# Rows of maxima by four turnings and two transfers, maxima 20 steps ahead, products of the first dense group among the second block's transpositions

## The chip, the core and the metric

The kernel runs on one core of a Trainium2 chip. The metric is the device time of one execution in microseconds (us). Five engines work beside each other, each on its own list of instructions in order: TensorE (PE: matrix products; PEld: the loading of their weights), VectorE (DVE), ScalarE (ACT), GpSimd (POOL) and SyncE (SP, which issues nearly all transfers here).

## The reference

The input x has 2048 rows of 512. It is normalised to xn, and two branches are multiplied: attention with 32 heads of 16 that share one key head and one value head, and a dense layer pair with Mish between.

```
xn = layernorm(x)                              # 2048 x 512
q  = xn @ wq  (32 heads of 16);  k = xn @ wk;  v = xn @ wv      # one k, one v
p  = softmax(q k^T / 4)  over 2048 keys, for each head
s  = concat(p v) @ wo                          # 512 x 512
h  = xn @ w1 + b1                              # 1792 wide
a  = h * tanh(softplus(h))
g  = silu(a @ w2)
out = x + s * g
```

## The kernel before, in words

Queries are cut into four chunks of 512, heads into eight groups of four. One chunk with one group of heads is a *vector* v here; there are NU = 32 of them. A vector's scores are made twice.

- *Maxima* (`m_one`, product L1118, reduction L1122): queries on the partitions, 512 keys a product. DVE reduces each product to one maximum per row. A vector has 64 of them: on each of two sides a (partitions 0 to 63 and 64 to 127) 32.
- *Scores* (`score`, product L1090, exponential L1095): keys on the partitions, 512 queries a product; ACT takes the exponential. 64 a vector. The softmax needs the maximum subtracted, and it comes in through the product itself: two more rows of the query tile `qt` (row 48 and 49 of each side) hold the negated maximum in two parts, and the key tile holds ones there.

`c_rows(v)` brings the maxima of a vector into these rows, in four pieces: `reduce` (the last maximum over four key blocks), `parts` (two instructions that split it), `turn` (DVE's transposition in blocks of 32x32, from queries on the partitions to queries along the row; L1151) and `move` (SP transfers from `cr` into `qt`, L1161). The first score of a vector waits for them.

The loop over 512 *steps* (16 a vector) issues in each step four scores, four value products (`pv`, L1176; each shows as two instructions in the trace) and the four maxima (two a side) of a vector LEAD steps ahead, so with LEAD = 22 the maxima of vector v end 6 steps ahead of its first score. Between them it lays the *dense* products (`xps`: query projections, both dense layers and the output projection). Inside the loop they run as two halves of 64 rows on the two sides, 4, 6 or 8 halves a step (`waves`), or 16 halves in two steps of a *unit* of four steps (`unit`), or none where no dense group is ready. `top_rows` issues one piece of `c_rows` a step (two per half unit). The last LEAD steps (`tail_pair`, two steps a pair) have no maxima.

Ahead of the loop stands a *lead*: normalisation, transpositions of x (`xp`, L315, four blocks of 512 rows: c = 0 to 3), key and value projections (`kp`, L356), the first query projections and 2 x LEAD maxima a side. A planner lays it out as it builds the program: each task has an engine, a cost and its predecessors; the planner keeps a clock T for each engine and issues the task that can start earliest. Kind "M" is a pair of maxima, kind "X" up to three dense products in whole (L118), and where nothing is ready it issues a product whose result is not used (`keep_warm`, L1431 before). A task with `fill=True` (transpositions of blocks 1 to 3) gets a `keep_warm` in front if no dense group is open. When the 32 maxima a side of vector 0 are issued, the planner sets tasks for `c_rows(0)` and the time `cdone` at which its rows will have landed; the lead ends at `cdone` less 0.4 us, and not before `min(m_next)` reaches 2 x LEAD.

Tile names in the rows: `qt` queries, `ks` keys, `m` and `e` the products of maxima and scores, `mb` the maxima, `mp` their parts, `cr` the turned rows, `pts` exponentials (and at the start x), `xps`, `wop` and `y2ps` banks of dense products, `hb` the first dense layer's output, `ws`, `wq`, `wbs` weights in two parts, `raw*` weights as loaded.

## Time and profile before

| | |
|---|---|
| median of 3 runs | 1561.91 us (1559.70 to 1562.19) |
| profiled execution, its own time | 1561.58 us |
| its span, first to last instruction | 1559.8 us |
| mean granted TensorE clock | 0.998 of full speed |
| busy: PE, DVE, ACT, POOL | 99%, 86%, 83%, 41% of the span |
| maxima, scores, value products | 2048, 2048, 2048 (x2 in the trace) |
| reduction of one maximum (L1122), mean | 683 ns listed |
| exponential of one score (L1095), mean | 607 ns listed |

The profile is one execution. A row of the timeline merges like instructions in a row; its length counts to the end of the last, while the next row may start before that, since instructions overlap by part of their length. The time that a row costs the engine is therefore the distance from its start to the next row's. Starts are counted from the first instruction of the span. In brackets stands how long the engine stood idle ahead of the row, and what ended that.

### The profile page before, as it was taken

The numbers are of one execution on the slowest core, as the hardware profiler recorded it, in microseconds if no ns is written. First come the engines' busy times: TensorE is split into PE (matmuls) and PEld (weight loads), VectorE is DVE, ScalarE is ACT, GpSimd is POOL, SyncE is SP. The second block draws the span as 40 slices with busy tenths as digits, with TensorE's granted clock in tenths as the row PEclk, the third lists the DMA queues.
The fourth block names the chain that finished last, engine by engine and source line by source line (L and its number), as shares of the span: only waits on it lengthen the run. The fifth ranks groups of instructions, "written<-read, shape, count | busy, mean of one in ns | idle before, by whom it ended". The sixth has DMA issues, their size and how long they took to land.

```text
span 1559.8 us, 31423 instructions
## 1 busy us (share of the span) xinstructions
PE 1548.8 (99%) x11715; PEld 864.1 (55%) x11715; DVE 1348.1 (86%) x2280; ACT 1292.6 (83%) x2509; POOL 636.3 (41%) x668
## 2 busy tenths in 40 slices
PE   9999999999999999999999999999999999999998
PEld 6555655655555565565545556555554555655644
DVE  7998888889989988888998988888889999888854
ACT  6588888789888778977989788897788878878796
POOL 4787349366356203331625422163152323314122
PEclk9999999999999999999999999999999999999999
DMA  6334134133231303212113220321321213131020
GB/s 199 104 133 139 46 111 139 30 113 112 87 111 49 108 16 113 72 24 100 52 58 111 92 92 17 104 69 58 111 59 38 100 58 105 30 99 32 19 71 34
DMA packets 71955, 125.47 MB, mean 80 GB/s; under 512 B 19742, under 2 KB 33356, under 8 KB 71804
## 3 DMA queue, kind: packets, MB, share of 16 engines
q1 hardware_dynamic: 71372, 122.68, 24.9%
q8 instruction: 93, 1.52, 0.4%
q10 hardware_dynamic: 432, 0.79, 0.1%
q14 instruction: 58, 0.48, 0.1%
HBM read 75.57 MB, written 26.21 MB: 65 GB/s over the span
## 4 chain that ended last, share of the span: by engine, by line
PE 98%; DVE 1%; ACT 0%; DMA 0%; issue 0%
PE xps L122 45%; PE pv L1176 32%; PE m L1118 10%; PE e L1090 7%; PE xps L118 1%; DVE mb L1122 1%; PE warm L1344 1%; PE kp L356 0%; PE xp L315 0%; PE wop L122 0%; ACT pts L1095 0%; PE y2ps L122 0%; DMA ks<-ks 0%; PE wop L118 0%; ACT hb L808 0%; ACT xt L324 0%
## 5 line engine op out<-in xcount | busy, mean ns | idle before, releaser
L1122 DVE TENSOR_REDUCE mb<-m 128x1 f32<-128x512 f32 x2048 | 1266.2, 683 | 164.2 <-PE m L1118 129.0
L1095 ACT ACTIVATE pts<-e 128x512 f32<-128x512 f32 x2048 | 1064.8, 607 | 218.3 <-PE e L1090 164.0
L1118 PE MATMUL m<-ks,qt 48*128 48x512 f32 (+1 forms) x2048 | 842.3, 422 | 1.2 <-DMA ks<-ks 1.2
L1090 PE MATMUL e<-qt,ks 64*128 64x512 f32 x2048 | 750.9, 406 | 0.2 <-ACT pts L1095 0.2
L1176 PE MATMUL pv<-pts,vaug 128*32 128x512 f32 x4096 | 529.9, 603 | 0.0
L1118 PEld LDWEIGHTS m<-ks,qt 48*128 48x128 f32 (+1 forms) x2048 | 371.1, 185 | 79.5 <-DVE mb L1122 41.4
L1090 PEld LDWEIGHTS e<-qt,ks 64*128 64x128 f32 x2048 | 375.8, 186 | 29.9 <-ACT pts L1095 16.3
L122 PE MATMUL xps<-wbs,act 64*128 64x512 f32 x1270 | 324.6, 399 | 0.0
L122 PE MATMUL xps<-xt,ws 64*128 64x512 f32 x1128 | 312.3, 409 | 1.7 <-ACT pts L1095 0.9
L122 PEld LDWEIGHTS xps<-xt,ws 64*128 64x128 f32 x1128 | 194.4, 185 | 185.7 <-ACT pts L1095 123.3
L122 PEld LDWEIGHTS xps<-wbs,act 64*128 64x128 f32 x1270 | 227.0, 184 | 99.5 <-ACT pts L1095 26.8
L1176 PEld LDWEIGHTS pv<-pts,vaug 128*32 128x32 f32 x4096 | 88.3, 108 | 152.5 <-issue 144.5
L175 POOL TENSOR_TENSOR hb<-hb,t 128x512 f32<-128x512 f32 x56 | 72.2, 1289 | 163.2 <-ACT t L827 89.4
L185 POOL TENSOR_SCALAR t<-t 128x512 f32<-128x512 f32 x56 | 34.4, 614 | 181.5 <-ACT t L814 181.4
L122 PE MATMUL xps<-xt,wq 64*128 64x512 f32 x336 | 93.0, 409 | 0.0
L122 PEld LDWEIGHTS xps<-xt,wq 64*128 64x128 f32 x336 | 57.9, 185 | 55.4 <-ACT pts L1095 37.7
L175 POOL TENSOR_TENSOR oc<-oc,sc 128x512 f32<-128x512 f32 (+1 forms) x16 | 20.6, 1290 | 152.5 <-DMA qt<-qh 49.8
L122 PE MATMUL xps<-wbs,ot_all 64*128 64x512 f32 x288 | 79.3, 408 | 0.0
L122 PEld LDWEIGHTS xps<-wbs,ot_all 64*128 64x128 f32 x288 | 49.5, 184 | 46.9 <-ACT pts L1095 28.5
L175 POOL TENSOR_TENSOR act<-hb,act 128x512 fp32r<-128x512 f32 x56 | 72.1, 1288 | 4.7
L175 POOL TENSOR_TENSOR hb<-hb,u 128x512 f32<-128x512 f32 x56 | 72.2, 1289 | 4.4
L175 POOL TENSOR_TENSOR u<-u,t 128x512 f32<-128x512 f32 x56 | 71.9, 1284 | 4.7
(164 smaller groups left out, 878.6 us busy)
## 6 DMA issues: line engine op xcount, KB each, us to landing
wbs<-w SPq DMA_DIRECT2D x39, 512.0 KB
ws<-w SPq DMA_DIRECT2D x36, 512.0 KB
qt<-qh SPq DMA_DIRECT2D x256, 32.0 KB
w<-wbs SPq DMA_DIRECT2D x14, 512.0 KB
wq<-wq SPq DMA_DIRECT2D x14, 512.0 KB
wbs<-wo SPq DMA_DIRECT2D x12, 512.0 KB
rawws<-in_dram SPq DMA_DIRECT2D x20, 256.0 KB
w<-ws SPq DMA_DIRECT2D x10, 512.0 KB
```

The source lines that it names most:

```text
L118: self.pe.matmul(ps, self.lhs(), self.rhs(), start=(self.k == 0), stop=(self.k == self.tot - 1))
L122: i = self.pe.matmul(ps, self.lhs()[o], self.rhs()[o], start=(self.k == 0 and self.halves == 0), stop=(self.k == self.tot - 1 and self.hal ...
L175: eng.tensor_tensor(out=o, in0=a, in1=b, op=op)
L185: pool.tensor_scalar(o, o, lim, 0.0, op0=ALU.min, op1=ALU.max)
L1090: pe.matmul(e, ks[o:o + 64, P * k:P * (k + 1)], q[o:o + 64, p], start=True, stop=True)
L1095: x = act.activation(dst, e, AF.Exp, scale=0.25)
L1118: pe.matmul(m, q[o, p, P * t:P * (t + 1)], ks[o, C * kb:C * (kb + 1)], start=True, stop=True)
L1122: return dve.reduce_max(out=mb_of[v][:, kb, z:z + 1], in_=m, axis=AX.X)
L1176: pe.matmul(o[32 * j:32 * j + 32], vaug[:, k], pt, start=(k == 0), stop=(k == 15))
L1344: pe.matmul(warm, qts[0][:, 0, 0:P], qts[0][:, 0], start=True, stop=True)
```

## The change

Four things change. LEAD goes from 22 to 20 (with a term of the query projections' due time adjusted so that it stays where it was). `turn` becomes four transpositions of 32 partitions each, that write side by side into a tile of 32 partitions x 128, in place of one of 128 x 32. `move` needs two transfers a vector (one a side, of 16 rows of 512 bytes) in place of eight of 16 rows of 128 bytes. And in the planner a dense product is issued ahead of each `fill` task while a dense group is open and its clock stands below 27.0 us; the costs of `c_rows(0)` in the planner follow the new forms.

```diff
-LEAD = 22
+LEAD = 20
...
-                     [lambda: 32 * (4 * c + b) - LEAD - 18, lambda: xt_done.get(c)])
+                     [lambda: 32 * (4 * c + b) - LEAD - 20, lambda: xt_done.get(c)])
...
         def turn():
-            cr = w["cr"] = sb.tile([P, 32], F32, tag="cr", name=f"cr{v}", bufs=2)
-            dve.transpose(cr, f(mp[:, :, 1:3]).rearrange("p a s z -> p a (s z)"))
+            cr = w["cr"] = sb.tile([32, P], F32, tag="cr", name=f"cr{v}", bufs=2)
+            for b in range(4):
+                z = slice(32 * b, 32 * b + 32)
+                dve.transpose(cr[:, z], f(mp[z, :, 1:3]).rearrange("p a s z -> p a (s z)"))
...
             for a in range(1, -1, -1):
                 r = 64 * a + 48
-                for b in range(4):
-                    sp_at(0.68)
-                    sp.dma_start(f(q[r:r + 2]).rearrange("o p (t b n) -> b o (p t) n", b=4, n=32)[b],
-                                 cr[32 * b + 16 * a:32 * b + 16 * a + 16])
+                sp_at(0.68)
+                sp.dma_start(f(q[r:r + 2]).rearrange("o p (t n) -> o (p t) n", n=P), cr[16 * a:16 * a + 16])
...
-                r1 = task("DVE", 0.9, lambda: (r[0](), r[1](), r[2]()))
+                r1 = task("DVE", 1.2, lambda: (r[0](), r[1](), r[2]()))
...
-                    cdone[0] = now[0] + 4 * 0.65 + 2.0
-                task("SP", 5.2, move, [r1])
+                    cdone[0] = now[0] + 2 * 0.65 + 2.0
+                task("SP", 1.3, move, [r1])
...
             plan[e].remove(k)
-            if k.fill and cur["g"] is None and not waiting:
+            if k.fill and cur["g"] is not None and s < 27.0:
+                fill(1)
+            elif k.fill and cur["g"] is None and not waiting:
                 keep_warm()
```

How the order of instructions moves is shown at three places. The first is PE at the end of the lead (`m` maxima, `xps` dense products, L118 in whole and L122 in halves). Before:

```order
L118 MATMUL xps<-xt_175,ws_833 128x512 x3
L1118 MATMUL m_0_8_955<-ks,qt_78 128x512
L1118 MATMUL m_1_8_958<-ks,qt_78 128x512
L1118 MATMUL m_0_9_963<-ks,qt_78 128x512
L1118 MATMUL m_1_9_966<-ks,qt_78 128x512
L118 MATMUL xps<-xt_175,ws_833 128x512 x6
L1118 MATMUL m_0_10_982<-ks,qt_78 128x512
L1118 MATMUL m_1_10_985<-ks,qt_78 128x512
L1118 MATMUL m_0_11_988<-ks,qt_78 128x512
L1118 MATMUL m_1_11_991<-ks,qt_78 128x512
```

And in the changed kernel, with the first rows of the loop behind it:

```order
L118 MATMUL xps<-xt_175,ws_842 128x512 x12
L1431 MATMUL warm<-qt_79 128x512 x2
L122 MATMUL xps<-xt_175,ws_929 128x512
L1118 MATMUL m_1_8_980<-ks,qt_78 128x512
L122 MATMUL xps<-xt_175,ws_929 128x512
L1090 MATMUL e_0_0_1_984<-qt_77,ks 128x512
```

Eight maxima have left the lead; the twelve dense products of that group now follow each other, and two products without use stand where the first dense group of the loop waits for its bank.

The second place is SP's queue ahead of the first rows of maxima (`ks<-ks` copies the keys of block 3 to the other side, `raw*` loads weights). Before:

```order
L537 DMA rawws_762<-in_dram 128x4x128
L539 DMA rawwb_774<-in_dram 128x512
L372 DMA ks<-ks 48x256 x2
L537 DMA rawws_881<-in_dram 128x4x128
L1161 DMA qt_77<-cr_911 2x8x32 x8
```

And now:

```order
L537 DMA rawws_775<-in_dram 128x4x128
L372 DMA ks<-ks 48x256 x2
L539 DMA rawwb_792<-in_dram 128x512
L537 DMA rawws_890<-in_dram 128x4x128
L1162 DMA qt_77<-cr_917 2x8x128 x2
```

The copy of the keys has moved ahead of one weight load, and eight transfers have become two.

The third place is PE in the loop, step 8: before, and then in the changed kernel.

```order
L1118 MATMUL m_1_28_1337<-ks,qt_78 128x512
L122 MATMUL xps<-xt_175,xtw 128x512
L1090 MATMUL e_8_0_1_1341<-qt_77,ks 128x512
L122 MATMUL xps<-xt_175,xtw 128x512
L1118 MATMUL m_1_29_1345<-ks,qt_78 128x512
L122 MATMUL xps<-xt_175,xtw 128x512
L1090 MATMUL e_8_1_1_1349<-qt_77,ks 128x512
```

```order
L1118 MATMUL m_0_24_1312<-ks,qt_78 128x512
L1090 MATMUL e_8_0_1_1315<-qt_77,ks 128x512
L1118 MATMUL m_0_25_1318<-ks,qt_78 128x512
L1090 MATMUL e_8_1_1_1321<-qt_77,ks 128x512
L1118 MATMUL m_0_26_1324<-ks,qt_78 128x512
L1090 MATMUL e_9_0_1_1327<-qt_77,ks 128x512
```

No dense product lies between them any more; four steps in a row are like that, since the planner has no dense group ready there.

Over the whole program PE's lists differ as follows. Steps with maxima: before 333 with 6 halves, 26 with 4, 4 with 8 and 62 half units with 16; now 331, 26, 4, 62 and the four without any. Pairs of the tail: before eight with 9 or 10 halves, then two with 13 and one with none; now eight with 9 or 10, then two with 18. The lead has 84 dense products in both, 100 maxima up to the loop's first value products before and 92 now, and seven products without use more.

## Rows read from the trace of the kernel before

**Rows 1.** The page: busy us of each engine, then the chain that ended last.

```profile
PE 1548.8 (99%) x11715; PEld 864.1 (55%) x11715; DVE 1348.1 (86%) x2280; ACT 1292.6 (83%) x2509; POOL 636.3 (41%) x668
...
PE 98%; DVE 1%; ACT 0%; DMA 0%; issue 0%
```

**Rows 2.** Timeline, PE, value products, 388:403 and 538:548 us (start, length, line, form).

```profile
394.27 1.06 PE L1176 MATMUL pv<-pts,vaug 128*32 128x512 f32 x8
397.12 1.06 PE L1176 MATMUL pv<-pts,vaug 128*32 128x512 f32 x8
399.82 1.07 PE L1176 MATMUL pv<-pts,vaug 128*32 128x512 f32 x8
...
539.79 1.06 PE L1176 MATMUL pv<-pts,vaug 128*32 128x512 f32 x8
542.86 1.07 PE L1176 MATMUL pv<-pts,vaug 128*32 128x512 f32 x8
```

**Rows 3.** Timeline, PE, end of the lead.

```profile
61.84 0.83 PE L1118 MATMUL m<-ks,qt 64*128 64x512 f32 x4 [1.19 <-DMA ks<-ks]
...
75.21 0.73 PE L1118 MATMUL m<-ks,qt 64*128 64x512 f32 x4
75.88 1.66 PE L118 MATMUL xps<-xt,ws 128*128 128x512 f32 x6
...
79.88 0.50 PE L122 MATMUL xps<-xt,ws 64*128 64x512 f32 x1 [0.78 <-ACT hb L808]
```

**Rows 4.** Timeline, SP's queue, 54 to 78 us.

```profile
58.15 0.33 SPq L539 DMA_DIRECT2D rawwb<-in_dram  x1
58.57 1.15 SPq L372 DMA_DIRECT2D ks<-ks  x2
```

**Rows 5.** Timeline, DVE, 18 to 86 us.

```profile
28.89 3.68 DVE L1122 TENSOR_REDUCE mb<-m 128x1 f32<-128x512 f32 x6 [1.57 <-PE m L1118]
...
56.09 0.85 DVE L175 TENSOR_TENSOR ks<-kp,ks 16x256 fp32r<-16x256 f32 x2
...
62.34 9.66 DVE L1122 TENSOR_REDUCE mb<-m 128x1 f32<-128x512 f32 x16 [0.49 <-PE m L1118]
...
72.76 0.21 DVE L1151 STREAM_TRANSPOSE cr<-mp 128x32 f32<-128x32 f32 x1
```

**Rows 6.** Windows: stretch, its length, busy us of the engines, then PEclk.

```profile
24.00:29.00 5.00, 4.99 (x20) 3.13 (x19) 3.01 (x7) 4.45 (x13) 2.12 (x5) 0.66 0.24 58
```

**Rows 7.** Timeline, DVE, behind the turning of vector 5.

```profile
307.36 4.28 DVE L1122 TENSOR_REDUCE mb<-m 128x1 f32<-128x512 f32 x7 [0.98 <-PE m L1118]
```

**Rows 8.** Timeline, SP's queue, the transfers of vector 5.

```profile
306.40 5.29 SPq L1161 DMA_DIRECT2D qt<-cr  x8
```

**Rows 9.** Timeline, PE, the first score of vector 5.

```profile
313.12 0.40 PE L1090 MATMUL e<-qt,ks 64*128 64x512 f32 x1
```

**Rows 10.** Timeline, PE, value products of the tail, 1518 to 1549 us.

```profile
1525.47 1.92 PE L1176 MATMUL pv<-pts,vaug 128*32 128x512 f32 x16
1529.91 1.92 PE L1176 MATMUL pv<-pts,vaug 128*32 128x512 f32 x16
1534.93 1.92 PE L1176 MATMUL pv<-pts,vaug 128*32 128x512 f32 x16
1539.99 1.92 PE L1176 MATMUL pv<-pts,vaug 128*32 128x512 f32 x16
1544.43 3.64 PE L1176 MATMUL pv<-pts,vaug 128*32 128x512 f32 x32
```

**Rows 11.** Timeline, DVE, the tail, 1518 to 1549 us.

```profile
1520.36 0.69 DVE L882 TENSOR_TENSOR y<-xps,y 128x512 f32<-128x512 f32 x1 [4.08 <-PE wop L122]
...
1525.17 3.34 DVE L1218 RECIPROCAL sc<-sc 64x512 f32<-64x512 f32 x1
...
1537.44 0.69 DVE L175 TENSOR_TENSOR y<-y,e 128x512 f32<-128x512 f32 x1
1548.63 0.42 DVE L1240 COPY os<-pv 128x256 f32<-128x256 f32 x1 [10.50 <-ACT os L1239]
```

## The prediction

> **What bounds the kernel now.** I read the page first: PE is busy 99% of the span and the chain that ended last is PE for 98% [rows 1]. So time is saved only where PE waits, where it does something without use, or where a step costs more than its products. To see which of these the change touches, I counted instructions by step in the two orders and took the price of a step from PE's timeline: the distance between two blocks of value products. A step with 6 dense halves costs 397.12 - 394.27 = 2.85 us, one with 4 costs 399.82 - 397.12 = 2.70, one with 8 costs 542.86 - 539.79 = 3.07 [rows 2]. The two halves from 6 to 8 cost 0.22 (0.11 each, PE's rate), those from 4 to 6 only 0.15, so something beside PE's products sets a floor near 2.7. Then I read the lead, where PE still waits, engine by engine [rows 3 to 6], and the tail, where ACT's exponentials set 4.44 us a pair [rows 10].
>
> **The change part by part.** The sum is made against the profiled execution's own 1561.58 us, 0.33 below the median of the runs; 1559.8 of it is the span and 1.8 lies around it.
>
> *Eight maxima leave the lead.* At its end PE does four maxima in 75.88 - 75.21 = 0.67 us [rows 3], and two such rows go: -1.3. The wait for the bank at 79.88 (0.78, until ACT has emptied it) stays, and the two products without use fit in it. The transfers of vector 0 do not take its place: the turning starts at 72.76 [rows 5], three more turnings add 0.6, two transfers at 5.29 / 8 = 0.66 each [rows 8] end by 75.1, and the loop would now start near 79.88 - 2.5 = 77.4.
>
> *The keys' copy goes ahead of a weight load.* SP issues it at 58.57, right behind a load at 58.15 [rows 4]; its data are there at 56.09 + 0.85 = 56.94 [rows 5], and one load of 0.33, like that at 58.15, still stands in front: 57.3. So it starts 1.3 us earlier, and PE's wait of 1.19 us at 61.84 goes [rows 3]. What is late next is DVE, which gains only its own 0.49 us [rows 5]; the reductions then run 16 in 9.66, or 0.604 each, without a gap. If PE must go at DVE's pace this is worth 0.5; since it has free banks between the two, I take -1.2.
>
> *Products among the transpositions.* [...] Five dense products are moved in front of these transpositions (from later in the lead; five products without use stand there instead). If the clock stays up the gain is at most 1.7 us; if it falls all the same, five products at 1.66 / 6 = 0.28 [rows 3] cost 1.4. DVE's idle 1.57 us at 28.89 [rows 5] is the part that could pass on. But ACT is busy for 4.45 of these 5 us [rows 6], and the maxima over key block 1 need what it makes there, so what PE gains is given back at their first product. I take 0, with -1.7 and +1.4 as ends. [...]
>
> *The loop.* It has two steps more with maxima: four without dense halves come, two with 6 go. A step without any isn't in the trace. It can't be under DVE's four reductions, 4 x 0.604 = 2.42, and hardly over the 2.85 of a step with 6; I take the nearest row, 2.70. That is 4 x 2.70 - 2 x 2.85 = +5.1, between +4.0 and +5.7.
>
> *The tail.* One pair less. Before, the last three intervals are 5.02, 5.06 and 4.44 = 14.52 us, from 1529.91 to 1544.43 [rows 10], for pairs with 13, 13 and no halves. Now two pairs with 18 stand for them; the eight with 9 or 10 stay, at 4.44 each as the one from 1525.47 to 1529.91. 18 halves cost 5.04 + 5 x 0.11 = 5.6. In the last pair ten are free, as the pairs at 4.44 show, and eight cost 0.9: 5.3. So 14.52 becomes 10.9: -3.6. The ends: 5.04 + 4.44 (all free) gives -5.0, 5.6 + 4.44 + 18 x 0.11 = 12.0 (none free in the last) -2.5.
>
> *Four turnings.* One took 0.21 us [rows 5]. Three more are at most 0.6 us of DVE for each of 32 vectors. In units DVE idles 0.98 us right behind the turning [rows 7], which covers it. In a single step DVE has 2.85 - 2.42 = 0.43 of room, and 0.82 for the turning is 0.39 too much; the three banks between PE and DVE hold back 1.8 us of reductions, so the next step makes it up. I take 0.01 a vector, +0.3 in all; the ends are 0 and 31 x 0.39 = +12. [...]
>
> *Two transfers.* Six issues of 0.66 us less for each vector [rows 8] free SP, which isn't on the path: 0. The time that they save is what LEAD = 20 spends. By the order, four vectors are now the tightest, with five maxima between their turning and their first score; vector 5 before has nine and takes 313.12 - 306.40 = 6.7 us from the first issue to its first score [rows 8, 9], with eight transfers in it and no wait. Four maxima are one step, so 6.7 - 2.85 - 0.6 = 3.2 remain. The first side's transfer is 0.66 long; the copy of keys, a larger one, was used 61.84 - 59.72 = 2.1 after its issue ended [rows 3, 4]. Together 2.8: it fits, by 0.4. I take 0, with +4 (four vectors, 1 us each) as the end.
>
> *The end of the tail.* The reciprocal at L1218 now stands behind the last addition to y (L882), which moves from the sixth-last pair to the third-last. Before, 1525.17 to 1537.44 + 0.69 is 13.0 us from that reciprocal to the last gate on y [rows 11]. Now it starts about 0.7 behind the third-last pair's value products (the addition stands 0.7 ahead of them, 1520.36 to 1521.03, and two instructions of 0.7 come first), so it is through at 13.7; DVE's copy for the last vector stands at 1548.63 - 1534.93 = 13.7 by the same count [rows 10, 11], and 1.4 later with the two longer pairs. So it costs nothing, by 1.4 us; +1 if it doesn't hold.
>
> The sum: -1.3 - 1.2 + 0 + 5.1 - 3.6 + 0.3 = -0.7, so **1560.9 us**.
>
> **The rivals.** *Faster: the clock stays up and the lead's gain is kept.* For it: 1.7 us lost at half clock, DVE idle 1.57 us behind it [rows 5, 6], and a step without dense halves may cost 2.42 rather than 2.70 (-1.1). Against it: ACT is full there. Time: 1560.9 - 1.7 - 1.1 = 1558.1.
>
> *Slower: the turnings stall PE.* Place: the single steps in which a vector is turned, where the maxima wait for a bank. Against it: the banks' 1.8 us and DVE's 0.98 in units [rows 7]. For it: 0.39 us over the step. Half of this uncovered, 0.2 x 31 = 6.2, gives 1560.6 + 6.2 = 1566.8. It makes the kernel slower than before from 1.0 / 31 = 0.03 us a vector on.
>
> *The rows come late.* If the transfers land 1 us later than counted, four vectors wait: 1564.9. The last pieces of the tail could add 1 in the same way.
>
> *The change does nothing for the path at all* is only the case in which lead, loop and tail cancel, which the forecast already nearly is.
>
> **How the numbers follow.** What a measurement of this kernel can tell from no change is about 0.2%, 3.1 us: below 1558.8 or above 1565.0. The forecast has 0.60, with its own range of 1558.9 to 1562.9 from the ends of loop and tail. The faster rival has 0.25 (nearly all below 1558.8), the turnings 0.09, the late rows and the tail's end 0.06 (a third above 1565.0). So faster 0.25, same 0.64, slower 0.11, and the range is 1557.3 to 1564.4, which leaves out the far end of either rival.
>
> **What would show it.** In the profile after: PE's gap ahead of the maxima at about 61 us gone, the loop's first score 2 to 3 us earlier; four value-product distances of 2.4 to 2.85 us at steps 8 to 11; the next to last tail distances near 5.6 and 5.3; the granted clock from 24 to 29 us near 1.0 if the products hold it; steps with a turning at 2.85 as before; DVE's copy at the end not waiting for DVE's own reciprocal. The prediction is wrong if steps with a turning grow, if first scores wait for `cr`, or if the first 80 us change by more than 4 us.

## The result, and the profile after

The changed kernel takes 1565.07 us (median of 9 runs, 1564.84 to 1565.51), the kernel before 1559.96 beside it (9 runs, 1559.70 to 1563.39): ratio 1.0026, 95% interval 1.0016 to 1.0036. It is slower by about 0.26%, and 1565.07 lies 0.7 us above the range of the forecast. The profiled execution took 1565.04 us. Four disturbed runs of the experiments (2397.66 us of after_rev, 3572.86 of dup0, 2060.81 and 7013.09 of the kernel before) are in no median below.

The page after, to be read beside [rows 1]: DVE has 19 us more, in 96 instructions more, which are three more turnings for each of 32 vectors; PE stays at 99%.

```profile
PE 1551.0 (99%) x11722; PEld 862.5 (55%) x11722; DVE 1366.9 (87%) x2376; ACT 1295.0 (83%) x2509; POOL 637.8 (41%) x668
```

The timeline of PE at the end of the lead (start, length, line, form, idle time ahead in brackets) answers to [rows 3]: four maxima at 60.04 without the wait of 1.19 us, and the loop's first product at 77.00 in place of 79.88.

```profile
60.04 0.73 PE L1118 MATMUL m<-ks,qt 64*128 64x512 f32 x4
...
76.45 0.49 PE L1431 MATMUL warm<-qt 128*128 128x512 f32 x1 [0.54 <-ACT hb L808]
77.00 0.49 PE L122 MATMUL xps<-xt,ws 64*128 64x512 f32 x1
```

The window of the transpositions answers to [rows 6]: the granted clock (third number from the end) is 1.00 where it was 0.66.

```profile
24.00:29.00 5.00, 4.89 (x26) 3.07 (x25) 3.73 (x6) 4.92 (x15) 1.74 (x3) 1.00 0.18 43
```

The value products on PE's timeline answer to [rows 2] and [rows 10]. The four steps without dense halves take 3.04, 3.23, 2.71 and 2.71 us; the last two pairs, with 18 halves each, 5.18 and 5.19.

```profile
98.80 1.07 PE L1176 MATMUL pv<-pts,vaug 128*32 128x512 f32 x8
101.84 1.06 PE L1176 MATMUL pv<-pts,vaug 128*32 128x512 f32 x8
105.07 1.07 PE L1176 MATMUL pv<-pts,vaug 128*32 128x512 f32 x8
...
1537.52 1.92 PE L1176 MATMUL pv<-pts,vaug 128*32 128x512 f32 x16
1542.70 1.92 PE L1176 MATMUL pv<-pts,vaug 128*32 128x512 f32 x16
...
1547.89 3.64 PE L1176 MATMUL pv<-pts,vaug 128*32 128x512 f32 x32
```

The time is lost in a place that the forecast held free. A single step that holds a vector's turning is longer in 20 of 31 vectors. Here are DVE and then PE in one of them.

```profile
1272.88 2.48 DVE L1122 TENSOR_REDUCE mb<-m 128x1 f32<-128x512 f32 x4
1275.29 0.83 DVE L1153 STREAM_TRANSPOSE cr<-mp 32x32 f32<-32x32 f32 x4
1276.05 2.43 DVE L1122 TENSOR_REDUCE mb<-m 128x1 f32<-128x512 f32 x4
1278.73 1.29 DVE L1122 TENSOR_REDUCE mb<-m 128x1 f32<-128x512 f32 x2 [0.25 <-PE m L1118]
1280.05 0.69 DVE L175 TENSOR_TENSOR y<-xps,y 128x512 f32<-128x512 f32 x1
```

```profile
1274.17 1.06 PE L1176 MATMUL pv<-pts,vaug 128*32 128x512 f32 x8
...
1276.44 0.40 PE L1090 MATMUL e<-qt,ks 64*128 64x512 f32 x1
1276.75 0.49 PE L1118 MATMUL m<-ks,qt 48*128 48x512 f32 x1
...
1277.17 1.07 PE L1176 MATMUL pv<-pts,vaug 128*32 128x512 f32 x8
```

The weights of that last product of maxima are loaded just before it (PEld's timeline):

```profile
1276.74 0.18 PEld L1118 LDWEIGHTS m<-ks,qt 48*128 48x128 f32 x1 [0.34 <-DVE mb L1122]
```

From the turnings' start to the next maximum 0.76 us pass; one turning took 0.21 [rows 5]. The first maximum behind them ends at about 1276.05 + 0.68 = 1276.73, and PE's fourth product of maxima in the step starts at 1276.75, 0.31 behind the product ahead of it where the rhythm is 0.23; its weight load has waited 0.34 for DVE. The step takes 1277.17 - 1274.17 = 3.00 us for 2.85 [rows 2].

### The profile page after: what moved, and what is told of

Same layout as the page of the kernel before. It is cut to its first block, busy times and chain, and to the rows that moved or that the text cites. A ratio compares the mean times of both kernels' runs of the same rounds, so it can differ in the third digit from the quotient of the medians.

```text
span 1563.2 us, 31137 instructions
## 1 busy us (share of the span) xinstructions
PE 1551.0 (99%) x11722; PEld 862.5 (55%) x11722; DVE 1366.9 (87%) x2376; ACT 1295.0 (83%) x2509; POOL 637.8 (41%) x668
## 4 chain that ended last, share of the span: by engine, by line
PE 97%; DVE 2%; ACT 1%; DMA 0%; issue 0%; SPq 0%; DVEq 0%
PE xps L122 44%; PE pv L1176 32%; PE m L1118 11%; PE e L1090 6%; PE xps L118 1%; DVE mb L1122 1%; PE wop L122 0%; PE kp L356 0%; PE xp L315 0%; DMA pts<-in_dram 0%; ACT pts L1095 0%; PE y2ps L122 0%; PE warm L1431 0%; PE wop L118 0%; DVE cr L1153 0%
## 5 line engine op out<-in xcount | busy, mean ns | idle before, releaser
L122 PE MATMUL xps<-wbs,act 64*128 64x512 f32 x1270 | 324.0, 399 | 0.1
L122 PE MATMUL xps<-xt,ws 64*128 64x512 f32 x1128 | 312.3, 409 | 1.0 <-ACT pts L1095 1.0
L122 PEld LDWEIGHTS xps<-xt,ws 64*128 64x128 f32 x1128 | 194.3, 185 | 184.9 <-ACT pts L1095 123.2
L122 PEld LDWEIGHTS xps<-wbs,act 64*128 64x128 f32 x1270 | 227.3, 184 | 97.2 <-ACT pts L1095 26.8
L122 PE MATMUL xps<-xt,wq 64*128 64x512 f32 x336 | 93.1, 409 | 0.0
L122 PEld LDWEIGHTS xps<-xt,wq 64*128 64x128 f32 x336 | 57.9, 185 | 55.0 <-ACT pts L1095 36.9
L122 PE MATMUL xps<-wbs,ot_all 64*128 64x512 f32 x288 | 79.4, 408 | 0.0
L122 PEld LDWEIGHTS xps<-wbs,ot_all 64*128 64x128 f32 x288 | 49.5, 184 | 47.1 <-ACT pts L1095 28.5
```

The costliest lines, as they stand in the source:

```text
L122: i = self.pe.matmul(ps, self.lhs()[o], self.rhs()[o], start=(self.k == 0 and self.halves == 0), stop=(self.k == self.tot - 1 and self.hal ...
```

## The experiments

Times of kernels on one chip are compared with runs of the kernel before beside them. Some runs of the kernel before have a lower mean granted clock (the last section); "at equal clock" means those at 0.999 or 1.000. Theory A: the price is the four turnings in DVE's time of a step. Theory B: it is the new order. What the further letters mean stands in the expectations.

**The turnings alone, and what of them costs.** Four kernels on before's order.

```
# turn4_same: the change's turn() and move() in the kernel before, nothing else
# cut4: one turning cut by partitions, the eight transfers stay
+            for b in range(4):
+                z = slice(32 * b, 32 * b + 32)
+                dve.transpose(cr[z], f(mp[z, :, 1:3]).rearrange("p a s z -> p a (s z)"))
# same4: the old turning four times over
+            for b in range(4):
+                dve.transpose(cr, f(mp[:, :, 1:3]).rearrange("p a s z -> p a (s z)"))
# turn4_split22: as turn4_same, two turnings each in two successive steps
+            for _ in range(4 if v == 0 else 2):
+                b = w["b"].popleft()
-            rowq.extend([r[0], r[1], lambda r=r: (r[2](), r[3]())])
+            rowq.extend([r[0], r[1], r[2], lambda r=r: (r[2](), r[3]())])
```

> The kernel before with the four turnings and the two transfers of the change alone: maxima still 22 steps ahead, no products in front, the planner's costs of before. Theory A (in the trace of the changed kernel a step of single score groups that holds four serial turnings, 0.76 to 0.84 us on DVE, takes about 3.00 us where such a step takes 2.85 and a step of the kernel before with one turning of 0.20 us takes 2.85 too; about 20 such steps, and two at 0.3 to 0.4): about 3 us slower than before (ratio 1.0015 to 1.0025). Theory B (the turnings have their room beside PE, and what the changed kernel lost came from maxima 20 steps ahead, by the four steps without dense halves): no difference, 0.9995 to 1.0005.

Measured 1565.51 us against 1560.38, ratio 1.0031 (1.0019 to 1.0042): the loss is there in full without maxima 20 steps ahead or products in front (the planner only lays some units of the loop at other steps, 17 to 20 and 157 to 160, which comes to -0.2 us). Theory A, but dearer than its 3 us.

> The kernel before with its one turning of 128 partitions cut into four of 32, each written to the partitions it is read from, so that the eight transfers and everything else stay as they are. Theory A (the turnings' time on DVE alone is the price): the four take 0.76 to 0.84 us one behind the other, single steps that hold them 3.00 instead of 2.85, and the run is about 3 us slower than before, as the kernel with four turnings and two transfers. Theory B: no difference. A third way (the loss comes with the two transfers, which read rows of 32 partitions in another pattern): this kernel as before, the one with two transfers slower.

1570.95, ratio 1.0064 (1.0051 to 1.0078). The transfers are innocent; turnings that also write to four groups of partitions are dearer still (1279.12 - 1278.20 = 0.92 us to the next maximum; 25 steps with a turning hold 9.8 us more than in the kernel before). That maximum starts 0.03 us after the turnings' end (1278.20 + 0.89), where in the changed kernel it starts 0.07 before it (1275.29 + 0.83 against 1276.05). It writes to partitions from 0 on, as in the changed kernel the last turning does, while here the last turning wrote to those from 96 on; whether that is why was not tried.

```profile
1278.20 0.89 DVE L1153 STREAM_TRANSPOSE cr<-mp 32x32 f32<-32x32 f32 x4
1279.12 2.48 DVE L1122 TENSOR_REDUCE mb<-m 128x1 f32<-128x512 f32 x4
```

> The kernel before with its turning of 128 partitions written four times over into the same tile (three of them superfluous), so that all four start at partition 0. What tells apart is the time from one to the next: if turnings that start at different partitions of a bank of 32 wait for each other and those that start at the same one follow without that wait, the four take clearly under the 0.76 us of the changed kernel's four (say 0.3 to 0.5 us) and the kernel loses under 1.5 us; if a turning is 0.19 to 0.20 us whatever stands before it, they take 0.8 us and the kernel is about 3 us slower, as with four of 32 partitions.

1568.36, ratio 1.0050 (1.0038 to 1.0063): 1277.45 - 1276.59 = 0.86 us for four. But they stand 0.25 us apart (the four are 0.94 long together, one 0.20), so each starts after the end of the one ahead, and they write the same tile; whether that or the partitions is why, this run doesn't tell, though it was made for it. dup0 and dupq below do.

> As the kernel with four turnings and two transfers at 22 steps ahead, but the four of a vector stand two and two in successive steps. Theory A: two turnings, 0.4 us, are 0.2 more in a step than before had; if the loss begins at once with each 0.1 us it comes to the same 3 us, spread on twice the steps; if the step has 0.25 us of slack (DVE idled 0.25 us behind a turning in the kernel before), nothing is lost: 0 to 0.5 us slower than before. Theory B: no difference either, and none in the undivided version.

1563.12, ratio 1.0016 (1.0007 to 1.0025); at equal clock 1561.6 against 1559.9. On DVE's timeline both pairs are over in 0.44 and 0.35 us, and no step with a turning is longer. What is left, 1.7 us for the 0 to 0.5 expected, lies in other steps (the last microsecond, below).

```profile
1269.29 0.40 DVE L1157 STREAM_TRANSPOSE cr<-mp 32x32 f32<-32x32 f32 x2
1269.73 2.48 DVE L1122 TENSOR_REDUCE mb<-m 128x1 f32<-128x512 f32 x4
1272.25 0.42 DVE L1157 STREAM_TRANSPOSE cr<-mp 32x32 f32<-32x32 f32 x2
1272.60 2.46 DVE L1122 TENSOR_REDUCE mb<-m 128x1 f32<-128x512 f32 x4
```

**Other ways to share it out, and the products in front.**

```
# after_13 (on the changed kernel) and turn4_13 (on turn4_same): one turning behind parts(), three a step later
+            rowq.extend([r[0], lambda r=r: (r[1](), r[2]()), lambda r=r: (r[2](), r[3]())])
# after_nofill: the changed kernel without
-            if k.fill and cur["g"] is not None and s < 27.0:
-                fill(1)
# fill_24: the kernel before with these two lines and s < 24.0
```

> The changed kernel with the four turnings of a vector in two successive steps: one behind the reductions to parts, three in the step after, nothing else moved. Theory A (a single step gives DVE about 0.6 us between two groups of four maxima, and each 0.1 us beyond that delays PE by about as much; the four at 0.77 overshoot it by 0.15 to 0.27 in 26 steps): the two steps now hold 0.63 and 0.58 us, so the 5 us are gone save 0 to 1: 1559.9 to 1561.5 us, at most 0.1% from the kernel before. Theory B (the loss of the changed kernel is rather in the four steps without dense halves and the order that 20 steps ahead bring): 1564 to 1565, as the changed kernel.

1565.08: nothing gained, and theory A in this form is wrong.

> The kernel before with four turnings (one behind the reductions to parts, three a step later) and two transfers of a vector, maxima 22 steps ahead. Theory A: no single step is longer by its turnings (at most 0.03 to 0.05 in some), so 0 to 1.3 us over the kernel before where both have the same granted clock: 1560 to 1561.5; the version with all four in one step gave 1565.5.

1565.74, ratio 1.0033 (1.0020 to 1.0046): no gain either. DVE shows why: beside four maxima a step of 2.85 us leaves 2.85 - 4 x 0.60 = 0.45 us, parts and a turning hold DVE 0.55 (1268.96 to 1269.51), the three 0.56 in the very next step, with no idle time between. DVE can be behind by some 0.15 more (an estimate: the limit near 0.6 given below, less 0.45); then PE waits. A step's 0.6 is not there twice running: these steps take 2.96.

```profile
1268.96 0.16 DVE L1144 TENSOR_REDUCE mp<-mp 128x16 fp32r<-128x16 f32 x1
...
1269.51 2.43 DVE L1122 TENSOR_REDUCE mb<-m 128x1 f32<-128x512 f32 x4
1271.97 0.63 DVE L1157 STREAM_TRANSPOSE cr<-mp 32x32 f32<-32x32 f32 x3
1272.53 2.43 DVE L1122 TENSOR_REDUCE mb<-m 128x1 f32<-128x512 f32 x4
```

> The changed kernel without products of the first dense group in front of the transpositions; its order then has no steps without dense halves, two more units and two more steps with four halves, and the tail fewer halves. If those products hold the clock up, the granted clock falls again between 24 and 29 us in some or all runs, and these are about 1.7 to 3.4 us longer than they would be. Four turnings unchanged, so their 5 us stay. The steps of the loop sum to the same by their prices (1406.1 against 1406.2 us), so with the clock kept: 1563.5 to 1565; with the clock fallen: 1565 to 1567. If the products were worth nothing: 1563.5 to 1564.5 in all runs.

1566.93; three runs at a clock of 1.000 took 1566.7 to 1566.9, two at 0.998 and 0.996 took 1567.7 and 1569.7. So the products in front don't cause the loss; the changed kernel has use of them. At the full clock this kernel is some 1.7 us slower than the changed one, where 1563.5 to 1565 was expected. Of that 1.1 is in the lead already, where the copy of the keys stands behind the weight load again and PE waits 1.07 us for it; the rest was not followed up.

> The kernel before with one product of the first dense group in front (begun before 24 us) and nothing else of the change; the order of the loop is that of before. If a product there holds the clock: the granted clock stays 1.00 from 24 to 29 us and every run is 1559.7 to 1560.2, with none near 1561.5 or 1563.5. If one product is too few: the same spread as the kernel before, 1559.7 to 1563.5.

1560.30 (11 runs, 1559.99 to 1561.19), all at 0.999 or more; ratio 0.9994 (0.9985 to 1.0002). The clock among the transpositions is 1.00 with a single product; the gain is only that the runs of lower clock are gone.

**The change without the four turnings.** Put back one turning and eight transfers; then share out a vector's rows otherwise.

```
# after_one8: turn() and move() of the kernel before in the changed kernel
# after_even: four turnings, one and then three; parts1() is the first reduction of parts()
+            rowq.extend([lambda r=r: (r[0](), r[4]()), lambda r=r: (r[1](), r[2]()), lambda r=r: (r[2](), r[3]())])
# same2: the kernel before with its turning twice over
+            for b in range(2):
```

> The changed kernel with the one turning of 128 partitions and the eight transfers of before put back; maxima 20 steps ahead, the products in front, and the order of all engines as in the changed kernel. Theory A (the four turnings cost the changed kernel 5 us and the rest of the change is worth about nothing): 1559.5 to 1561 us, no single step longer by its turning; 1560.9 is what was forecast for the whole change. Rival (the eight transfers take 5.3 us where two take 1.3, and with maxima 20 steps ahead the rows land too late): waits for rows in front of first scores in the four vectors whose margin was 1.0 us in the changed kernel, up to 3 us each, up to 12 us over Theory A. Theory B (the order is what costs): 1564 to 1565.

1564.78, ratio 1.0023 (1.0014 to 1.0032), a number that looks like theory B. The steps say otherwise: against the changed kernel the 20 steps with a turning lose 3.5 us and ten others 1.3, while four steps grow by 1.06 to 1.09 each, at the place that the rival had foretold and within its size (up to 3 us each): their first score waits for the eight transfers, issued from 399.31 for 5.30 us. PE and then SP's queue for vector 7:

```profile
400.57 1.07 PE L1176 MATMUL pv<-pts,vaug 128*32 128x512 f32 x8
...
403.17 0.47 PE L1090 MATMUL e<-qt,ks 64*128 64x512 f32 x1 [0.88 <-DMA qt<-cr]
...
404.76 1.07 PE L1176 MATMUL pv<-pts,vaug 128*32 128x512 f32 x8
```

```profile
399.31 5.30 SPq L1161 DMA_DIRECT2D qt<-cr  x8
```

> The changed kernel with the work on a vector's rows spread evenly over its three steps: the first reduction to parts stands beside the reduction ahead of it, the second beside one turning, and three turnings in the third step. Beside four maxima of 0.60 us each a single step of 2.85 us leaves DVE 0.45 us; from the durations read so far the three steps now hold about 0.54, 0.44 and 0.56 us. Theory A (a step stalls PE by what DVE holds above 0.45 us, less some 0.12 to 0.17 us that is taken up by the lag between the two engines): each overrun of 0.09 to 0.11 is taken up, no turning step longer by over 0.03 us: 1559.8 to 1561.3. If there is no such allowance and only the sum counts (0.2 us over in 31 vectors): 1564 to 1565.5.

1564.30: steps with a turning 2.91 in place of 3.00, 0.06 left in most of them, and 0.2 in two units; most of the loss stays. The number lies where the expectation put it if only the sum counts, but the steps show another way. The three turnings begin 1274.70 - 1272.19 = 2.51 us behind the start of the four maxima ahead, for 1275.29 - 1272.88 = 2.41 in the changed kernel, which the working had not.

> The kernel before with its turning written twice (one of them superfluous). Theory A: the step with the turnings holds 0.41 to 0.44 us beside its four maxima, under the 0.45 that a single step leaves, so no step is longer: 0 to 0.5 us over the kernel before, where four turnings written over each other cost 7.5. If each 0.2 us of DVE costs in proportion: 2.5 us over.

1561.72 (12 runs, seven of them at a lower clock), ratio 1.0003 (0.9994 to 1.0012); at equal clock 1560.12 against 1560.13, and no step longer. The two turnings hold DVE 1271.03 - 1270.59 = 0.44 us here, and that is free.

**Two checks of the rest.** Neither price paid, first by two queues, then by two steps in place of three in the four late vectors.

```
# after_pool: as after_one8, but
+                    e = (sp, pool)[b % 2] if not lead else sp
# after_mix: as after_one8, and
+            rowq.extend([lambda r=r: (r[0](), r[4]()), lambda r=r: (r[1](), r[2](), r[3]())] if vdone[0] in (7, 10, 18, 25)
+                        else [r[0], lambda r=r: (r[4](), r[1]()), lambda r=r: (r[2](), r[3]())])
```

> The changed kernel with the one turning put back and the eight transfers issued by two queues in turn, four by SP and four by POOL (the first vector's all by SP), so that the rows are there some 2.6 us sooner than with eight on SP, where first scores waited 1.1 us in four vectors. Theory C (two prices, each hiding the other: four turnings cost about 4.9 us of stalls in the changed kernel, eight transfers on one queue 4.3 us of late rows, and the rest of the change is worth nothing): no step with a turning is longer, no first score waits, 1560 to 1561.2 us. Rival (the order that 20 steps ahead bring costs 3 us or more by itself, and the steps only seem to recover): 1563 or more with no step longer by a turning or by late rows. If POOL issues slowly and its work is on PE's way, the steps with its work are longer instead, and the run says nothing on either.

1582.04. The transfers stand in POOL's own queue behind its other work (vector 4 is turned at 256.6, POOL issues its four from 264.75), and a first score waits 6.69 us. As written down, it tells nothing on the theories.

> The changed kernel with the one turning and its eight transfers on SP put back, and in the four vectors whose rows came 1.1 us late so (7, 10, 18 and 25) the rows made in two steps in place of three (first reduction to parts beside the reduction, second beside the turning). Theory C (four turnings 4.9 us, late rows 4.3 us, the rest of the change worth nothing): no step longer by a turning, no first score waits for rows, 1560.0 to 1561.2 us. Rival (20 steps ahead and the products in front cost 3 us or more by themselves): 1563 or more.

1560.52 (11 runs, 1560.08 to 1560.94), ratio 0.9998 (0.9989 to 1.0007). Theory C: the same order on PE as the changed kernel, without the turnings' price and without late rows, is 4.6 us faster than it and on a level with the kernel before. The step with a turning, PE, then DVE, then the weight load of PE's fourth product of maxima:

```profile
1270.33 1.07 PE L1178 MATMUL pv<-pts,vaug 128*32 128x512 f32 x8
1271.33 0.50 PE L1118 MATMUL m<-ks,qt 48*128 48x512 f32 x1
...
1272.83 0.40 PE L1118 MATMUL m<-ks,qt 48*128 48x512 f32 x1
...
1273.17 1.06 PE L1178 MATMUL pv<-pts,vaug 128*32 128x512 f32 x8
```

```profile
1271.45 0.20 DVE L1153 STREAM_TRANSPOSE cr<-mp 128x32 f32<-128x32 f32 x1
1271.90 2.48 DVE L1122 TENSOR_REDUCE mb<-m 128x1 f32<-128x512 f32 x4 [0.25 <-PE m L1118]
1274.73 1.29 DVE L1122 TENSOR_REDUCE mb<-m 128x1 f32<-128x512 f32 x2 [0.35 <-PE m L1118]
1275.94 0.68 DVE L175 TENSOR_TENSOR y<-xps,y 128x512 f32<-128x512 f32 x1
```

```profile
1272.64 0.18 PEld L1118 LDWEIGHTS m<-ks,qt 48*128 48x128 f32 x1
```

The fourth product of maxima stands 1.50 us behind the step's first, and it takes the bank of that first one, since there are three. The maximum that frees the bank ends at 1271.90 + 0.68 = 1272.58: 0.25 ahead of the product, but only 0.06 ahead of its weight load. In the changed kernel it is this load that waits 0.34 us for DVE.

**Why four turnings are served one by one.** Three superfluous turnings behind the one of before, into a tile that nothing reads, without waits among them; the two kernels differ in the partitions that the three read.

```
+            cd = sb.tile([32, P], F32, tag="cd", name=f"cd{v}", bufs=2)
+            for b in range(1, 4):
+                z = slice(32 * b, 32 * b + 32)
# dup0
+                dve.transpose(cd[:, z], f(mp[0:32, :, 1:3]).rearrange("p a s z -> p a (s z)"))
# dupq
+                dve.transpose(cd[:, z], f(mp[z, :, 1:3]).rearrange("p a s z -> p a (s z)"))
```

> The kernel before with three more turnings of 32 partitions behind its one, each from partitions 0 to 31 into a tile that nothing reads, with no wait between them. If a turning that starts at the partition where the one ahead of it started needn't wait for that one's end, the three follow at clearly under 0.19 us each (0.06 to 0.12), the four take 0.4 to 0.55 us and the loss is 0 to 2 us. If turnings are served one by one whatever they read, 0.19 us each, 0.77 in all, and 5 us of loss as with four turnings in the change.

1560.32, ratio 1.0003 (0.9993 to 1.0013): four turnings and no loss. On DVE they take 1267.74 - 1267.30 = 0.44 us:

```profile
1267.30 0.20 DVE L1151 STREAM_TRANSPOSE cr<-mp 128x32 f32<-128x32 f32 x1
1267.42 0.34 DVE L1155 STREAM_TRANSPOSE cd<-mp 32x32 f32<-32x32 f32 x3
1267.74 2.48 DVE L1122 TENSOR_REDUCE mb<-m 128x1 f32<-128x512 f32 x4
```

> As the kernel with three more turnings of partitions 0 to 31, but the three read partitions 32 to 63, 64 to 95 and 96 to 127. By every theory 0.19 us each, 0.77 us for the four, and 4.5 to 6 us slower than before, since the steps that hold them go from 2.85 to 3.00; against the other kernel it tells whether the start partition matters.

1566.41, ratio 1.0036 (1.0023 to 1.0049), with 1274.01 - 1273.21 = 0.80 us:

```profile
1273.21 0.20 DVE L1151 STREAM_TRANSPOSE cr<-mp 128x32 f32<-128x32 f32 x1
1273.44 0.63 DVE L1155 STREAM_TRANSPOSE cd<-mp 32x32 f32<-32x32 f32 x3
1274.01 2.43 DVE L1122 TENSOR_REDUCE mb<-m 128x1 f32<-128x512 f32 x4
```

The same number, size and target of instructions: only the group of partitions that each reads from decides between 0.44 and 0.80 us, and between no loss and 6. In dupq the three start 0.03 us after the end of the turning ahead (1273.21 + 0.20 = 1273.41, then 1273.44) and are 0.63 us long together; in dup0 they start 0.08 before it (1267.30 + 0.20 = 1267.50, but 1267.42) and are 0.34 long.

**The last microsecond.** Eleven steps without a turning are 0.12 to 0.14 us longer in the changed kernel than in after_mix, 1.4 us in all. In them DVE's addition to y comes late: in the fence of the result it starts at 1280.05, 1.32 us behind the two maxima's start and after their end (1278.73 + 1.29 = 1280.02); in after_mix 1275.94 - 1274.73 = 1.21 behind, before their end (1276.02). The same steps of before's order are longer in turn4_same, cut4, dupq, turn4_13 and turn4_split22, whose last turning reads partitions 96 to 127, and in none of same2, same4 and dup0, whose last one starts at partition 0.

```
# after_rev: the changed kernel; split22_rev: turn4_split22 with deque((3, 2, 1, 0))
-            for b in range(4):
+            for b in (3, 2, 1, 0):
```

> The changed kernel with its four turnings in the opposite order, the last one reading partitions 0 to 31. In the changed kernel eleven steps without a turning are 0.12 to 0.14 us longer than in the kernel with the one turning put back; in them DVE begins an addition to y 0.12 us late. Theory D (an instruction whose input in that memory starts in another group of 32 partitions than that of the last one to read it waits for the end of everything ahead; the maxima read PSUM, so the first to read SBUF behind the turnings is that addition, and the last turning read group 3): the eleven steps fall back to 2.87 to 2.99 (-1.4 us in all), while the first turning, which now starts in group 3 behind maxima, begins about 0.12 later, and the 20 steps with a turning grow by 0 to 0.14 more (up to +2.8): 1563.7 to 1566.5. Rival (the eleven steps are longer for a lag that PE and DVE carry on from the turning): they stay at 2.99 to 3.11.

1566.5 (four runs, 1566.04 to 1567.14), ratio 1.0034 (1.0021 to 1.0048). The eleven steps are shorter again by 0.10 to 0.14, and the 20 steps with a turning are at 3.12 to 3.24, 2.6 us more together. On DVE the turnings start 1276.28 - 1273.76 = 2.52 behind the four maxima's start, 0.11 later than in the changed kernel and now after the maxima's end (1273.76 + 2.48 = 1276.24); the addition is on time, 1.21 behind:

```profile
1273.76 2.48 DVE L1122 TENSOR_REDUCE mb<-m 128x1 f32<-128x512 f32 x4
1276.28 0.84 DVE L1153 STREAM_TRANSPOSE cr<-mp 32x32 f32<-32x32 f32 x4
...
1279.73 1.29 DVE L1122 TENSOR_REDUCE mb<-m 128x1 f32<-128x512 f32 x2 [0.25 <-PE m L1118]
1280.94 0.68 DVE L175 TENSOR_TENSOR y<-xps,y 128x512 f32<-128x512 f32 x1
```

> The kernel with maxima 22 steps ahead and four turnings in two pairs, with the order of the groups turned round (3, 2, then 1, 0). Theory D: the eight steps without a turning at 3.00 to 3.12 where the kernel before has 2.88 to 3.00 go back (-1.0 us); each pair's first turning is held too and the pair takes some 0.5 to 0.56 us, over the 0.45 that a step leaves by 0.05 to 0.11, which the lag takes up or not (0 to +2 us): 1559.9 to 1562 where the clock is the same. Rival: the eight stay as they were.

1560.44, ratio 0.9996 (0.9987 to 1.0005); at equal clock 1560.29 against 1560.32. The steps that are longer in turn4_split22 (ten and one unit, where the expectation counted eight) are shorter again by 0.12 to 0.14, the ten at 2.87 to 2.99, 1.4 us in all. Of the steps with a turning one is 0.08 longer, the others are not: four turnings and two transfers can be had for nothing, in two pairs of which the last reads partitions 0 to 31. Both runs agree with theory D, and after_rev with both signs: the turnings 0.11 us later, the addition 0.11 earlier than in the changed kernel. The maxima read PSUM, so the turnings' last group is still the last that read SBUF when the addition comes.

## Why the prediction was wrong

**The step that failed is "Four turnings"**, of which the prediction said: "the three banks between PE and DVE hold back 1.8 us of reductions, so the next step makes it up. I take 0.01 a vector, +0.3 in all". By the steps that after_mix wins back it was 3.5 us in 20 steps with a turning and 1.4 in eleven others: 4.9, or 0.16 a vector. The overrun itself was right (0.43 us of room and 0.82 for the turnings; the runs show 0.45 and 0.76). What was wrong is the cover. Three banks do not hold back 1.8 us here: PE's fourth product of maxima needs the very bank whose maximum stands first behind the turnings, and its weight load comes 1272.64 - 1271.33 = 1.31 us into the step. Beyond one turning's 0.20 us DVE has 0.25 idle and 0.06 to that load, not 1.8. So 0.44 us of turnings cost nothing (same2, dup0, split22_rev), and more is passed to PE: a step is longer by 0.15 for 0.76, 0.18 for 0.80 (dupq), 0.27 for 0.86 (same4), 0.37 for 0.92 (cut4), which points to a limit near 0.6 (an estimate from these four; no run lies between 0.44 and 0.76 with all its turnings in one step). The 1.4 us in the eleven other steps, where the addition comes 0.11 us late, the prediction did not have at all.

**The rival "the turnings stall PE"** had place and price: 0.2 a vector, 1566.8. It was given a chance of 0.09. The sign that the prediction named for itself, that steps with a turning grow, came. The trace of before had DVE's idle time in a single step, 0.24 us behind the turning; the working gave it away for the 1.8 us.

```profile
1268.68 0.20 DVE L1151 STREAM_TRANSPOSE cr<-mp 128x32 f32<-128x32 f32 x1
1269.12 2.48 DVE L1122 TENSOR_REDUCE mb<-m 128x1 f32<-128x512 f32 x4 [0.24 <-PE m L1118]
```

**The other terms.** Without the turnings' price and without late rows the same order takes 1560.52, and the sum was 1560.9. That this agrees is in part luck, since some of its terms were off against each other (profiled executions):

- The lead: first value products 2.3 us sooner, from 86.86 to 84.56; -2.5 was forecast for maxima and copy. With the clock held in the kernel before (fill_24) they are at 85.81, so 1.05 of it is the clock, for which 0 had been taken. After_nofill, at the full clock, has the eight maxima less but the copy still behind the load, and is at 85.66: the maxima gave 0.15 there, not 1.3 (0.73 at the loop's first product, 78.11 for 78.84; the loop's first steps take most of it back). The last 1.10 comes with the products in front, which also bring the copy forward, and PE's wait of 1.07 for it goes; 1.2 was forecast for the copy.
- The four steps without dense halves: 11.69 us, less two steps of 2.85, +6.0, for +5.1 and just beyond its end of +5.7. The first two, at 3.04 and 3.23, are above the 2.85 called an upper limit. In both the trace shows PE's fourth product of maxima waiting for DVE (at 101.08 and 104.12) and behind it the weight load of a score waiting for ACT (0.16 and 0.34 us, at 101.42 and 104.64), which has two activations of the dense layers between the exponentials; no run tried it.
- The tail: 46.34 us for ten pairs, where the eleven before took 50.01: -3.7, for -3.6. The last two took 10.4 for the 10.9 forecast, and a pair ahead of them 0.5 more than before.
- Two transfers: no first score waits in the changed kernel; in the four tightest vectors 1.0 us is between the last issue's end and the first score. Put back to eight, they are late by 1.1 in just these. The forecast gave them 3.2 us from the first issue to the first score and counted on 2.8; they had 2.4 (400.77 to 403.14 in vector 7), and that was enough.
- The end of the tail: the copy at L1240 waits for ACT, as before, and DVE is idle 0.87 us ahead of it. Nothing, as forecast.
- What remains of the difference of 3.5 us between the profiled executions (-1.4) lies in other steps of the loop, whose order is new, and was not followed up.
- Two slips in the prediction's arithmetic change nothing: four turnings at 0.21 are 0.84 and not 0.82, and the ends of loop and tail add to 1558.4 to 1562.6.

**The clock.** The faster rival counted on the clock staying up, which it does (1.00 from 24 to 29 us), and on 1.7 us kept, an estimate from [rows 6]: (1 - 0.66) x 5.00. At most 1.05 is kept at the first value products, and against the runs of before that have the full clock it is nothing.

## What to carry to other kernels

Ask of a buffer between two engines when its next slot is due, not how much it stores: the slack of a step is the time from the stall to the first slot that the faster engine needs again, and work beyond it costs time in every step that holds it (here 0.15 to 0.37 us for turnings of 0.76 to 0.92). Count a group of small vector instructions by where their inputs start (0.44 us for four here from one group of 32 partitions, 0.76 to 0.80 from four), and let the last of them read from the group that the next reader of the same memory starts in (0.10 to 0.14 us here in a step). And when undoing a part gives back nothing, compare step by step before dropping the theory: here two prices of 4.9 and 4.3 us had changed places.

## What the runs showed of the hardware

A turning of 128 partitions and three of 32 that read from its first group take 0.44 us together (dup0), four that read from four groups 0.76 to 0.80 (the changed kernel, dupq), and 0.92 if they also write to four groups (cut4). An instruction that comes later, with maxima between, still starts 0.11 us late when it is the next to read SBUF and its input starts in another group than that of the last one that read it: the addition in the changed kernel, 1.32 us behind the maxima for 1.21 in after_mix and after_rev, and the turnings in after_rev, 2.52 behind for 2.41 in the changed kernel.

The granted clock among the transpositions at 24 to 29 us differs from run to run of one kernel. In an execution of same2 that took 1563.46 us it was 0.55 there (first fence) and 0.996 in the mean of the span; with one dense product ahead of the transpositions, in fill_24, 1.00 (second). In the profiled execution of before it is 0.50 from 25 to 28 us, while PE does transpositions and maxima and is listed busy for 3.00 of the 3.00 us.

```profile
24.00:29.00 5.00, 4.98 (x17) 3.03 (x16) 2.76 (x6) 4.59 (x14) 2.08 (x5) 0.55 0.22 53
```

```profile
24.00:29.00 5.00, 4.02 (x22) 2.41 (x20) 3.61 (x7) 4.79 (x15) 1.84 (x4) 1.00 0.20 48
```

Of 107 runs of the kernel before beside the experiments, 66 had a mean clock of 0.999 or more (median 1560.29 us) and 41 less (1560.92 to 1564.41). Of the kernels with products in front and no long waits in the loop (the changed one, after_13, after_one8, after_even, after_mix, fill_24) all 63 had 0.999 or more; without them two of five runs of after_nofill had less. Why the clock falls while PE is listed busy is not shown: all 11 runs of fill_24, with one product ahead of the transpositions, have a mean of 0.999 or more, but so have 66 runs of before without that product (and the profiled one of dup0 has 1.00 from 24 to 29 us).
